# Linear attention and an ELU MLP on one core: a new order of the first loads, W1's first chunk by contraction tile, and a new order of all that follows

## Chip, cores and metric

One Trainium2 chip, one core. The metric is the device time of one execution in microseconds (us); every figure quoted as a time is the median of a kernel's runs. The span in a profile runs from the first to the last instruction and is about 1.8 us shorter than the time. All timed runs told here were in the fast state (two kernels have a single execution, e11 and e12, whose state is unknown), and all gave correct results.

## The reference

```python
def _attn_ref(q, k, v):                       # 8 batches, 8 heads, 576 tokens, 64
    q_s = np.exp(q - max over head_dim);  q_s /= sum over head_dim
    k_s = np.exp(k - max over tokens);    k_s /= sum over tokens
    kv = np.einsum('bhsd,bhse->bhde', k_s, v)
    return np.einsum('bhsd,bhde->bhse', q_s, kv)

def _moe_ref(x, w_in, w_out):                 # x: 4608 x 512, 512 -> 2048 -> 512
    h = x @ w_in
    g = np.where(h > 0.0, h, np.exp(np.minimum(h, 0.0)) - 1.0)
    return g @ w_out
```

(Shortened; `x` is the attention output with the heads side by side.)

## The kernel before

The program is a list of operations with their dependences, and a table `ORDER` that fixes the order on each engine by operation numbers. Two "halves" (`n`, four heads each) make a batch, 512 tokens make a block of the MLP. A "pitch" is the time from the start of one matmul to the start of the next, and "excess over the pitch" is what a start comes later than the usual pitch of its shape. Names: QS is exp(q) over its sum, qsT its transpose, VB the cast v, MBLK the normalised k-v product ("M"), XT the MLP's input (transposed attention output), GT the activated hidden layer, ESB its exponent, OSBX and OSB the outputs on their way out.

The start, and the loads of W1:

```python
        for n, t in ((0, "q"), (1, "q"), (0, "k"), (0, "v"), (1, "k"), (1, "v")):
            self.load(n, t, -40, "sp", follow=self.gpq)
            self.gpq = S.ops[-1]
            if (n, t) == (0, "k"):
                gate = S.ops[-1]
        loaded = S.ops[-1]
        for g0, g1, half in ((0, 3, 0), (0, 3, 1), (3, 5, None), (5, 8, None)):
            self.load_w1(g0, g1, half, -30, [gate, self.ident] if half == 0 else ())
            S.ops[-2].behind = loaded
        # ... stage1, transposes, k-v products, M for both halves ...
        self.side(C, -5, self.ao_mm(0, 0, C))      # product with M, one operation
        # ...
        for half in range(2):                      # MLP of block 0: contraction halves
            for g in range(3):
                self.hg_mm(0, g, turns[g], key, half)
```

Idle stretches of PE near the start are filled with spare matmuls on the identity, so that its clock "opens" early (the pitch of a spare matmul falls from 427 to 216 ns); their number comes from a schedule worked out when the kernel is built:

```python
                count = int((o.start - free - 150) / (430 if free == self.SPIN_FROM else 260))
```

The softmax here doesn't subtract the row's maximum and nothing guards it: scores larger than these inputs give would overflow.

## Time and profile before

| quantity, kernel before | value |
|---|---|
| time, 3 runs | 301.47 us (301.1 to 301.81) |
| span in the profile | 299.0 us |
| first MLP matmul (PS<-XT,W) | 14.95 us |
| first output matmul (PS<-W,GT), "first out" below | 30.70 us |
| from first out to the start of the last matmul | 265.02 us |

Up to first out lie the start, the MLP of block 0 and the loads of W1; after it everything else.

One stretch of PE's timeline (columns: start us, us, engine, line, operation, output<-inputs, size, count; in brackets idle time before it and what ended it), kernel before:

```profile
49.90 4.70 PE L547 MATMUL PS<-XT,W 128*128 128x512 f32 x20
54.98 1.19 PE L592 MATMUL PS<-W,GT 128*128 128x512 f32 x4 [0.39 <-DVE GT L582]
56.26 2.14 PE L547 MATMUL PS<-XT,W 128*128 128x512 f32 x8
```

PE stops before the four output matmuls because DVE has not yet written their GT. The gap over the usual pitch is 0.55 us here, and 0.25 more before the MLP matmuls at 56.26.

### The profile page before, as it was taken

The numbers are of one execution on the slowest core, as the hardware profiler recorded it, in microseconds if no ns is written. First come the engines' busy times: TensorE is split into PE (matmuls) and PEld (weight loads), VectorE is DVE, ScalarE is ACT, GpSimd is POOL, SyncE is SP. The second block draws the span as 40 slices with busy tenths as digits, with TensorE's granted clock in tenths as the row PEclk, the third lists the DMA queues.
The fourth block names the chain that finished last, engine by engine and source line by source line (L and its number), as shares of the span: only waits on it lengthen the run. The fifth ranks groups of instructions, "written<-read, shape, count | busy, mean of one in ns | idle before, by whom it ended". The sixth has DMA issues, their size and how long they took to land.

```text
span 299.0 us, 4421 instructions
## 1 busy us (share of the span) xinstructions
PE 287.1 (96%) x1851; PEld 234.5 (78%) x1851; DVE 189.5 (63%) x244; ACT 182.3 (61%) x212; POOL 21.7 (7%) x33
## 2 busy tenths in 40 slices
PE   0899999999999999999999999999999999999995
PEld 0487877677888888888888888888888888888885
DVE  3958935985898685894568855588427256655500
ACT  5858848988977967867755766534462423432411
POOL 0860145100000000000000000000000000000000
PEclk9999999999999999999999999999999999999999
DMA  7999998994498697289546327041312302004214
GB/s 260 387 398 389 390 391 262 240 371 157 118 247 259 141 338 181 71 263 266 175 116 164 88 66 186 2 99 37 86 36 51 70 2 53 0 0 107 64 41 105
DMA packets 35443, 49.96 MB, mean 167 GB/s; under 512 B 16352, under 2 KB 16608, under 8 KB 35424
## 3 DMA queue, kind: packets, MB, share of 16 engines
q1 hardware_dynamic: 29840, 34.15, 41.3%
q0 software_dynamic: 5504, 15.47, 16.3%
q8 instruction: 14, 0.23, 0.3%
q10 hardware_dynamic: 80, 0.07, 0.1%
q14 instruction: 5, 0.04, 0.1%
HBM read 36.70 MB, written 9.44 MB: 154 GB/s over the span
## 4 chain that ended last, share of the span: by engine, by line
PE 89%; DVE 4%; DMA 3%; ACT 1%; SPq 1%; issue 0%
PE PS L592 43%; PE PS L547 41%; PE PS L491 3%; DMA QT<-QS 2%; PE PS L460 2%; DMA QR<-in_q_dram 1%; DVE ZQ L376 1%; DVE QS L384 1%; PE PS L407 1%; SPq L634 1%; DVE XT L516 0%; DVE GT L582 0%; ACT QR L356 0%; ACT qsT L435 0%; ACT ESB L563 0%; DVE MBLK L473 0%
## 5 line engine op out<-in xcount | busy, mean ns | idle before, releaser
L592 PE MATMUL PS<-W,GT 128*128 128x512 f32 (+1 forms) x592 | 141.4, 386 | 0.4 <-DVE GT L582 0.4
L547 PE MATMUL PS<-XT,W 128*128 128x512 f32 x576 | 140.5, 391 | 0.7 <-DVE RZK L469 0.5
L547 PEld LDWEIGHTS PS<-XT,W 128*128 128x128 f32 x576 | 107.1, 188 | 24.0 <-DVE XT L516 0.9
L592 PEld LDWEIGHTS PS<-W,GT 128*128 128x128 f32 x592 | 107.7, 188 | 22.1 <-DVE GT L582 0.8
L563 ACT ACTIVATE ESB<-PS 128x1024 f32<-128x1024 f32 x72 | 73.7, 1027 | 64.7 <-PE PS L547 64.3
L580 DVE TENSOR_SCALAR ESB<-ESB 128x1024 f32<-128x1024 f32 x64 | 44.4, 695 | 67.0 <-ACT ESB L563 66.4
L582 DVE TENSOR_TENSOR GT<-ESB,PS 128x1024 fp32r<-128x1024 f32 x64 | 77.7, 1217 | 1.8
L624 ACT ACTIVATE OSB<-PS 128x512 f32<-128x512 f32 x31 | 18.2, 598 | 30.9 <-PE PS L592 30.6
L376 DVE TENSOR_REDUCE ZQ<-QR 128x18 f32<-128x1152 f32 x16 | 21.5, 1344 | 7.3 <-ACT QR L356 7.2
L513 ACT ACTIVATE XT<-PS 128x512 fp32r<-128x512 f32 (+6 forms) x32 | 19.5, 608 | 7.0 <-PE PS L491 6.5
L384 DVE TENSOR_TENSOR QS<-QR,RZQ 128x1152 f16<-128x1152 f32 x16 | 21.6, 1353 | 0.3
L356 ACT ACTIVATE QR<-QR 128x1152 f32<-128x1152 f32 x16 | 18.6, 1165 | 2.9 <-DMA QR<-in_q_dram 2.9
L360 ACT ACTIVATE KR<-KR 128x1152 bf16<-128x1152 f32 x16 | 18.5, 1160 | 3.0 <-DMA KR<-in_k_dram 3.0
L435 ACT ACTIVATE qsT<-QT 128x1152 fp32r<-128x1152 f16 x12 | 14.0, 1166 | 0.7 <-DMA QT<-QS 0.7
L369 ACT ACTIVATE VB<-VR 128x1152 bf16<-128x1152 f32 (+1 forms) x12 | 13.5, 1124 | 0.7 <-DMA VR<-in_v_dram 0.7
L491 PE MATMUL PS<-qsT,MBLK 128*128 128x320 f32 (+5 forms) x64 | 13.9, 303 | 0.0
L491 PEld LDWEIGHTS PS<-qsT,MBLK 128*128 128x128 f32 x64 | 11.7, 190 | 2.6 <-DVE MBLK L473 0.2
L576 DVE SCALAR_TENSOR_TENSOR GT<-PS,ESB 128x1024 fp32r<-128x1024 f32 x8 | 9.8, 1220 | 4.2 <-ACT ESB L574 4.2
L672 PE MATMUL PS<-ID 128*128 128x512 f16 x7 | 3.3, 590 | 7.5 <-ACT QR L356 7.5
L473 DVE TENSOR_TENSOR MBLK<-PS,RZK 64x128 fp32r<-64x128 f32 x32 | 9.2, 289 | 0.9
L574 ACT ACTIVATE ESB<-ESB 128x1024 f32<-128x1024 f32 x8 | 8.5, 1060 | 0.2
L469 DVE RECIPROCAL RZK<-PS 128x2 f32<-128x2 f32 x16 | 2.6, 164 | 8.7 <-PE PS L460 7.7
(29 smaller groups left out, 59.7 us busy)
## 6 DMA issues: line engine op xcount, KB each, us to landing
out_dram<-OSB SPq DMA_DIRECT2D x62, 128.0 KB, 2.4
QR<-in_q_dram SPq DMA_DIRECT2D x12, 576.0 KB, 5.3
KR<-in_k_dram SPq DMA_DIRECT2D x12, 576.0 KB, 5.6
VR<-in_v_dram SPq DMA_DIRECT2D x12, 576.0 KB, 5.6
W<-in_moe_w_out_dram POOLq DMA_DIRECT2D x4, 1024.0 KB, 18.9
QR<-in_q_dram POOLq DMA_DIRECT2D x4, 576.0 KB, 11.4
KR<-in_k_dram POOLq DMA_DIRECT2D x4, 576.0 KB, 11.6
VR<-in_v_dram POOLq DMA_DIRECT2D x4, 576.0 KB, 8.0
```

The lines of the kernel that those rows point to most:

```text
L356: S.add("act", t_act(1152, False), lambda e: e.activation(flat(q), flat(q), AF.Exp), key - 3, X=[f"qR{i}"], follow=self.table)
L360: S.add("act", t_act(1152, False), lambda e: e.activation(ek[:, :, :, :].rearrange("p h c d -> p (h c d)"), flat(k), AF.Exp), key - 2, X=[ ...
L376: S.add("dve", t_dve(1152), lambda e: e.tensor_reduce(self.ZQ[i][:, :, :].rearrange("p h c -> p (h c)"), q[:, :, :, :].rearrange("p h c d ...
L384: S.add("dve", t_dve(1152), lambda e: e.tensor_tensor(qso, q[:, :, :, :], rz, ALU.mult), key - 3, R=[f"qR{i}", f"RZQ{i}"], W=[f"QS{self.al ...
L491: last = e.matmul(P[:, y:y + n_], M[:, f, :], T[:, c0:c1, f * 64:f * 64 + 64], start=True, stop=True)
L513: S.add("act", t_act((h1 - h0) * n_, True), lambda e, dst=dst, src=src: e.activation(dst, src, AF.Copy), key, W=W, X=X)
L547: last = e.matmul(P[:, t * 512:(t + 1) * 512], self.W1[:, kc, tt * 128:(tt + 1) * 128], self.XT[:, kc, rc:rc + BLK], start=(kc == 0), stop ...
L563: S.add("act", t_act(1024, True), lambda e: e.activation(esb[:, :], P[:, :], AF.Exp), key, W=[f"E{i}"], X=banks)
L580: S.add("dve", t_dve(1024, 2), lambda e: e.tensor_scalar(esb[:, :], esb[:, :], 1.0, -1.0, ALU.min, ALU.add), key, X=[f"E{i}"])
L582: S.add("dve", t_dve(1024), lambda e: e.tensor_tensor(gt, esb[:, :], P[:, :], ALU.max), key, R=[f"E{i}"], W=gw, X=banks)
L592: last = e.matmul(dst, GT[:, jj, ts * 128:(ts + 1) * 128], self.W2[:, jj, c0:c1], start=(jj == 0), stop=(jj == 15))
L624: S.add("act", t_act(512, True), lambda e: e.activation(osb[:, :], src, AF.Copy), key, W=[f"O{i}0", f"O{i}1"], X=[f"b{bk}"])
```

## The change

Its intent: let the k-v product of half 0 start earlier (k second instead of third), and let the MLP begin on the first quarter of W1's first chunk instead of its first half. With both, all later orders were drawn up anew, so `ORDER` differs nearly everywhere. Core of the diff:

```diff
     "sp": (
-        "8 9 10 11 12 13 170 187 161 164 171 185 165 190 200 168 162 199 209 210 216 167 219 277 278 "
+        "8 9 10 11 12 13 197 178 195 171 172 181 200 180 177 175 209 219 210 174 220 226 229 325 287 "
 ... (all five engines' tables are new; numbers from about 50 on are shifted)
-        for n, t in ((0, "q"), (1, "q"), (0, "k"), (0, "v"), (1, "k"), (1, "v")):
+        for n, t in ((0, "q"), (0, "k"), (1, "q"), (0, "v"), (1, "k"), (1, "v")):
...
-            if (n, t) == (0, "k"):
+            if (n, t) == (1, "q"):
                 gate = S.ops[-1]
-        for g0, g1, half in ((0, 3, 0), (0, 3, 1), (3, 5, None), (5, 8, None)):
-            self.load_w1(g0, g1, half, -30, [gate, self.ident] if half == 0 else ())
+        for g0, g1, kcs in ((0, 3, (0,)), (0, 3, (1,)), (0, 3, (2, 3)), (3, 5, range(4)), (5, 8, range(4))):
+            self.load_w1(g0, g1, kcs, -30, [gate, self.ident] if kcs == (0,) else ())
...
-        self.side(C, -5, self.ao_mm(0, 0, C))
+        self.ao_parts(0, C, -5)
...
-        for half in range(2):
+        for kc in range(4):
             for g in range(3):
-                self.hg_mm(0, g, turns[g], key, half)
+                self.hg_mm(0, g, turns[g], key, kc=kc)
```

`ao_parts` issues the two matmuls of the product with M as two operations, so each releases its copy alone. The six first loads have the operation numbers 8 to 13 in both kernels.

## The prediction

> **What bounds the kernel now.** I read four views, from coarse to fine: the page's busy times, the busy table by stretches of time, then the timelines of PE and DVE for the first 17 us, and last the weight transfers from issue to landing.
>
> The page and the table by stretches (columns: stretch, its length, PE busy with its instructions, granted clock, DMA share, GB/s):
>
> ```profile
> PE 287.1 (96%) x1851; PEld 234.5 (78%) x1851; DVE 189.5 (63%) x244; ACT 182.3 (61%) x212; POOL 21.7 (7%) x33
> ...
> 14.95:24.75 9.80, 9.80 (x42) 1.00 1.30 397
> 24.75:30.33 5.58, 5.58 (x25) 1.00 1.24 388
> 30.33:46.95 16.62, 16.62 (x124) 1.00 1.13 379
> 46.95:60.00 13.05, 12.58 (x157) 1.00 0.98 242
> 60.00:76.00 16.00, 15.91 (x70) 1.00 0.71 245
> 76.00:100.00 24.00, 24.00 (x179) 1.00 0.75 197
> ```
>
> PE bounds it: idle for 299.0 - 287.1 = 11.9 us, of which 7.46 lie before its first instruction and 3 behind its last. From the first MLP matmul (14.95) to the last one PE has under 1 us of idle time. So the time is nearly "start of the MLP plus a fixed amount of PE work", and a change of the start moves the end one to one unless something else holds PE later. The second thing to see is the last column: up to 46.95 the transfers run at 379 to 397 GB/s, that is saturated too.
>
> The start, on PE:
>
> ```profile
> 7.46 2.31 PE L672 MATMUL PS<-ID 128*128 128x512 f16 x5 [7.46 <-ACT QR L356]
> 10.12 1.14 PE L407 MATMUL PS<-ID,QS 128*128 128x128 f16 x9 [0.34 <-DVE QS L384]
> 11.19 0.71 PE L460 MATMUL PS<-VB,KR 64*64 64x65 bf16 x36
> 11.83 0.61 PE L672 MATMUL PS<-ID 128*128 128x512 f16 x1
> 12.23 1.02 PE L407 MATMUL PS<-ID,QS 128*128 128x128 f16 x9
> 13.93 0.48 PE L460 MATMUL PS<-VB,KR 64*64 64x65 bf16 x36
> 14.95 1.17 PE L547 MATMUL PS<-XT,W 128*128 128x512 f32 x4 [0.53 <-DVE RZK L469]
> ```
>
> and on DVE:
>
> ```profile
> 10.27 1.36 DVE L384 TENSOR_TENSOR QS<-QR,RZQ 128x1152 f16<-128x1152 f32 x1
> 11.95 0.17 DVE L469 RECIPROCAL RZK<-PS 128x2 f32<-128x2 f32 x1 [0.32 <-PE PS L460]
> 12.16 0.61 DVE L473 TENSOR_TENSOR MBLK<-PS,RZK 64x128 fp32r<-64x128 f32 x2
> 12.80 0.76 DVE L372 CAST VB<-VR 128x576 bf16<-128x576 f32 x1
> 13.59 0.69 DVE L417 CAST qsT<-PS 128x512 fp32r<-128x512 f16 x1
> 14.20 0.68 DVE L516 CAST XT<-PS 128x512 fp32r<-128x512 f32 x1
> ```
>
> From QS of half 1 (ready at 11.63) DVE works almost without a gap until the XT copy at 14.88. The weights (issue, then the time to landing of those issued in a stretch):
>
> ```profile
> 8.41 5.08 POOL L336 DMA_DIRECT2D W<-in_moe_w_in_dram x8 [6.58 <-DMA KR<-in_k_dram]
> ...
> W<-in_moe_w_in_dram POOLq DMA_DIRECT2D x1, 384.0 KB, 5.2
> ...
> PEld PS L547 <- DMA W<-in_moe_w_in_dram: 0.3, 1, 0.3
> ```
>
> The first half of W1's first chunk lands at 8.41 + 5.2 = 13.6; the trace's landing records give 14.86 for the second half, which the first MLP matmul also needs. So two things release it within 20 ns: W1 at 14.86 and XT on DVE at 14.88 (the releaser in brackets, RZK, is only the last event on that counter). The last line is the load of W1's last columns: its record ends at 24.71, and PE starts on them at 24.75, with one pitch of 0.337 instead of 0.227 us. The input loads land at 4.69, 6.22, 8.11, 9.62, 11.11 and 12.61, about 1.5 us each (576 KB).
>
> **What the Trainium skill says.** "TensorE: Matmul & The Clock Gate", Part 1: the array runs at 1.2 GHz until a free-running activity window of about 3.4 us has been busy, then at 2.4; N=512 has a pitch of 426.7 ns cold and 215.7 warm, and the moment varies with the window's phase. The trace agrees: the first five filler matmuls on ID have a pitch of 427 ns, transposes 107 ns up to 12.87 and 57 ns after it. The f32r MLP matmuls have 227, not 216. The same page's table of specifications calls the queues of ScalarE, VectorE and GpSimdE strict FIFO; the DVE rows above are in program order throughout. "DMA: Bandwidth & Descriptors", Queues, rings and completion order: each DMA engine takes turns between the rows that have work, so an order inside one queue decides only who comes first, not how much is moved. The trace agrees: 390 to 406 GB/s whatever is under way. The Specifications there give 435 GB/s as the fabric's ceiling; no stretch of this trace goes above 412.
>
> **The change part by part.**
>
> Order q, k, q, v, k, v. The sixth transfer still lands at 12.61 and W1 is still gated on the third, so its issue stays at 8.41. k of half 0 takes the slot 6.22 and q of half 1 the slot 8.11. With ACT's 1.16 a pass: exp k0 6.25 to 7.41, exp q1 8.14 to 9.30. On DVE, QS of half 0 no longer stands behind the second reduce: reduce 5.91 to 7.26, reciprocal to 7.57, QS to 8.95 (before 10.06), 1.1 us sooner. But it buys nothing: the k-v product of half 0 needs the cast of v0, which still ends at 9.64 + 1.17 = 10.81. QS of half 1 is reduce 9.33 + 1.34, reciprocal 0.27, multiply 1.36, with 0.03 hops: 12.37, before 11.63. So 0.7 us are lost on the DVE queue, which was half of what set the start.
>
> DVE after that. The built order is RZK, MBLK first part, qsT copy, MBLK second part, V cast, XT copy. With the durations above: RZK 12.40 to 12.57, MBLK 12.60 to 12.88; the qsT copy needs the four transposes of half 1, which now come first in that group: 12.43 plus four pitches and a drain, about 12.85 at best. So 12.91 to 13.60, MBLK 13.63 to 13.92, V cast 13.95 to 14.70, XT 14.74 to 15.42. The k-v product of half 1 needs that cast and stands ahead of the MLP: 14.76 plus 0.35. First MLP matmul at best at about 15.1: 0.15 later than now.
>
> Filler matmuls. There are 12 now instead of 7: 3 before the transposes of half 0, 3 after them, 3 after the first k-v product, 3 after the transposes of half 1. Cold each takes 0.427, and they are in order with the real work. If the clock opens at 12.87 again: transposes from 9.01 to 9.97, three fillers to 11.27, k-v product from 11.4 (ready at 10.86) to 12.04, three fillers to 13.1; the transposes of half 1, ready at 12.43, start at 13.13, 0.7 late. The qsT copy then starts at 13.56 instead of 12.91, and everything behind it by as much: MLP at about 15.8. If the clock opens before about 11.6, the fillers fit and it stays 15.1. The opening could be anywhere from about 10 to 13.3 (window's phase), so on average about 0.25 us on top of the 0.15.
>
> W1 by contraction tile. First chunk now 2 x 192 KB, landing by about 13.6 instead of 14.86: 1.25 us won on the wait for weights, but off the path as DVE is later. The product with M in two parts lets ACT start its XT copy one pitch sooner (0.31), also beside the longer DVE chain. Two more descriptors' issues cost POOL 2 x 0.63 us, hidden: the last W1 is issued at 12.84 and lands 11.9 us later.
>
> End of W1. All bytes up to W1's last are the same, so it lands at about 24.7 again. Now PE meets it with 0.04 us to spare and loses 0.11 in the longer pitch. A later start regains that 0.11; an earlier one would wait there. Sum for the start: + 0.15 + 0.25 - 0.1 = + 0.3.
>
> The rest. The order of everything later is a new table (W2's chunks now come in pairs between the loads of q; the second block's first 32 MLP matmuls run in one piece). It moves no work in or out. The excess over the pitch between 46.95 and 76 is about 2 us in the trace (0.55 at 54.98, 0.25 at 56.26, 0.26 at 65.69, 0.16 at 74.35, and 0.11 at some restarts), so this can give or take some 0.5; I take 0 to - 0.1 for it.
>
> **The rivals.** (1) The intended gain in full: W1 1.25 us sooner gives an MLP start at 13.7. Against it: the DVE chain, and W1's last columns at 24.71, which would take it back; for the time it is worth 0.1 at most, 301.3. (2) Fillers cold to the end: + 0.9, 302.4. For it: the window in the trace before opened only at 12.87. (3) The new order of the middle wins or loses more than the start: 300.7 to 302.2; the DVE waits there are the only idle time left.
>
> **Range and chances.** 301.47 + 0.3 - 0.05 gives 301.7. The runs before spread by 0.7, the fillers by 0.9, the middle by about 0.5 each way: 8 in 10 from 300.8 to 302.6. Two per cent are 6 us, which nothing here reaches: faster 0.01, same 0.98, slower 0.01.
>
> **What would show it.** QS of half 1 ready at about 12.4; the qsT copy before MBLK's second part; first MLP matmul between 15.1 and 15.9 and released by the k-v product or XT, with W1's first tile landed at about 13.6; no longer pitch at W1's last columns, which land at about 24.7. I am wrong if the MLP starts before 14.9, if W1's last lands much before 24.7, or if the middle's PE waits change by more than 0.5 us.

## More of the kernel before

The output tiles of block 0 (OSBX) lie inside the buffer GT1, which block 1 writes, so a write of GT has to wait for the stores that still read it:

```python
        self.GT.append(a("GT1", [128, 16, BLK], F32R))
        # ...
        self.OSB0 = [at(f"OSBX{i}", [128, 512], F32, offset=base + 24576 + 2048 * i)
        # ...
        gw = [f"G{j % 2}_{g}"] + (self.early(g) if j == 1 else [])   # waits for OSBX's stores
```

The profiled execution took 300.83 us, less than any of the three timed ones.

## The result, and the profile after

The changed kernel took 300.68 us (300.4 to 301.11, 6 runs); the kernel before took 301.38 (6 runs) in the same comparison. The ratio is 0.9976, 95% interval 0.9963 to 0.9989. Ratios here are the mean time of one kernel's runs over that of the other's runs of the same rounds, so not quite the ratio of the medians. All outputs are right. It is within 2%, as predicted, but it is a small gain where a small loss was expected, and 300.68 lies just below the range (300.8 to 302.6).

The profiled execution happened to be the slowest of the six (span 299.3, before 299.0), so the profile cannot show the gain by its length. It is read by parts. The page of the changed kernel:

```profile
PE 287.9 (96%) x1856; PEld 234.4 (78%) x1856; DVE 187.5 (63%) x244; ACT 181.3 (61%) x212; POOL 22.8 (8%) x35
```

Five matmuls more are the five fillers more, two POOL instructions more are the two issues of W1. PE's timeline of the changed kernel up to the MLP:

```profile
8.93 1.14 PE L408 MATMUL PS<-ID,QS 128*128 128x128 f16 x9
9.86 1.49 PE L687 MATMUL PS<-ID 128*128 128x512 f16 x3
11.28 0.71 PE L461 MATMUL PS<-VB,KR 64*64 64x65 bf16 x36
11.93 0.85 PE L687 MATMUL PS<-ID 128*128 128x512 f16 x3
12.68 0.68 PE L408 MATMUL PS<-ID,QS 128*128 128x128 f16 x9
13.20 0.81 PE L687 MATMUL PS<-ID 128*128 128x512 f16 x3
14.19 0.73 PE L504 MATMUL PS<-qsT,MBLK 128*128 128x512 f32 x2 [0.18 <-DVE MBLK L474]
14.98 0.48 PE L461 MATMUL PS<-VB,KR 64*64 64x65 bf16 x36
15.39 0.50 PE L562 MATMUL PS<-XT,W 128*128 128x512 f32 x1
```

and DVE's:

```profile
11.26 1.36 DVE L385 TENSOR_TENSOR QS<-QR,RZQ 128x1152 f16<-128x1152 f32 x1
12.54 0.17 DVE L470 RECIPROCAL RZK<-PS 128x2 f32<-128x2 f32 x1
12.74 0.28 DVE L474 TENSOR_TENSOR MBLK<-PS,RZK 64x128 fp32r<-64x128 f32 x1
13.12 0.69 DVE L418 CAST qsT<-PS 128x512 fp32r<-128x512 f16 x1
13.84 0.29 DVE L474 TENSOR_TENSOR MBLK<-PS,RZK 64x128 fp32r<-64x128 f32 x1
14.16 0.76 DVE L373 CAST VB<-VR 128x576 bf16<-128x576 f32 x1
```

The transposes of half 0 come at 8.93 instead of 10.12, as intended. But half 1's QS ends at 12.62 (11.63 before), because its q now lands third, and then the DVE queue runs on without a gap: the V cast, the k-v product, the MLP at 15.39, which is 0.44 later than before. W1's first tiles landed at 13.38 and 13.84 and nobody waited for them.

The other end of the loads, from the table of waits of the changed kernel between 24 and 26 us (total, times, longest), and the stretch from there to first out (length, busy times of PE, PEld, DVE, ACT and POOL, clock, DMA share, GB/s):

```profile
PEld PS L562 <- DMA W<-in_moe_w_in_dram: 0.5, 1, 0.5
```

```profile
25.35:31.34 5.99, 5.95 (x28) 4.98 (x29) 4.87 (x6) 4.75 (x6) 0.00 (x0) 1.00 1.33 390
```

W1's last columns landed at 25.35 in this execution (24.70 and 25.16 in two others), and PE waited 0.26 us and 0.11 in a longer pitch. First out came at 31.34, 0.64 later than in the profile before. And yet the span is only 0.3 longer: the later work gave time back. PE's timeline of the changed kernel where the kernel before had its 0.55 us wait:

```profile
49.64 7.58 PE L562 MATMUL PS<-XT,W 128*128 128x512 f32 x32
57.06 2.06 PE L607 MATMUL PS<-W,GT 128*128 128x512 f32 x8
59.05 0.78 PE L461 MATMUL PS<-VB,KR 64*64 64x65 bf16 x72
```

All 32 MLP matmuls run in one piece and the eight output matmuls after them; GT is there in time, and there is no idle time before 57.06. The order has waits of its own for GT, though, as the next microseconds show:

```profile
60.11 3.94 PE L562 MATMUL PS<-XT,W 128*128 128x512 f32 x16 [0.28 <-DVE GT L597]
...
66.05 2.12 PE L562 MATMUL PS<-XT,W 128*128 128x512 f32 x8 [0.29 <-DVE GT L597]
```

They start 0.47 and 0.45 us over the pitch. The kernel before has no such wait near 60 and one of 0.26 at 65.69. So the 0.80 us of waits that went (0.55 and 0.25) were replaced in part.

### The profile page after: what moved, and what is told of

Same layout as the page of the kernel before. It is cut to its first block, busy times and chain, and to the rows that moved or that the text cites. A ratio compares the mean times of both kernels' runs of the same rounds, so it can differ in the third digit from the quotient of the medians.

```text
span 299.3 us, 4430 instructions
## 1 busy us (share of the span) xinstructions
PE 287.9 (96%) x1856; PEld 234.4 (78%) x1856; DVE 187.5 (63%) x244; ACT 181.3 (61%) x212; POOL 22.8 (8%) x35
## 3 DMA queue, kind: packets, MB, share of 16 engines
q0 software_dynamic: 5536, 15.47, 15.9%
## 4 chain that ended last, share of the span: by engine, by line
PE 84%; DMA 6%; DVE 4%; ACT 3%; POOL 2%; SPq 0%; issue 0%
PE PS L607 42%; PE PS L562 38%; DMA W<-in_moe_w_in_dram 4%; PE PS L492 2%; DMA QR<-in_q_dram 2%; POOL W L336 2%; PE PS L461 1%; DVE GT L597 1%; DVE GT L591 1%; ACT QR L357 1%; ACT OSBX L639 1%; DVE ESB L595 1%; DVE QS L385 0%; DVE ZQ L377 0%; ACT ESB L589 0%; DVE MBLK L474 0%
## 5 line engine op out<-in xcount | busy, mean ns | idle before, releaser
L526 ACT ACTIVATE XT<-PS 128x512 fp32r<-128x512 f32 (+6 forms) x32 | 19.4, 608 | 12.7 <-PE PS L492 7.7
L492 PEld LDWEIGHTS PS<-qsT,MBLK 128*128 128x128 f32 x60 | 11.0, 190 | 2.5 <-DVE MBLK L474 0.2
L492 PE MATMUL PS<-qsT,MBLK 128*128 128x320 f32 (+4 forms) x60 | 12.5, 296 | 0.0
L687 PE MATMUL PS<-ID 128*128 128x512 f16 x12 | 4.6, 508 | 7.3 <-ACT KR L361 7.3
L461 PEld LDWEIGHTS PS<-VB,KR 64*64 64x64 bf16 x576 | 5.7, 109 | 3.0 <-ACT VB L370 0.8
```

The lines of the kernel that those rows point to most:

```text
L492: last = e.matmul(P[:, y:y + n_], M[:, f, :], T[:, c0:c1, f * 64:f * 64 + 64], start=True, stop=True)
L526: S.add("act", t_act((h1 - h0) * n_, True), lambda e, dst=dst, src=src: e.activation(dst, src, AF.Copy), key, W=W, X=X)
```

## The experiments

To read them together, here is what the profile of each says of the two parts. "Runs" is the median of the timed runs, with their range; first out and "rest" (from first out to the last matmul's start) are from the trace.

| run | runs (us) | ratio to before, 95% | first MLP | first out | rest |
|---|---|---|---|---|---|
| before, medians in the comparisons | 300.91 to 301.38 | 1 | 14.95 | 30.70 | 265.02 |
| changed | 300.68 (300.4–301.11) | 0.9976 [0.9963, 0.9989] | 15.39 | 31.34 | 264.65 |
| e1 start only | 301.46 (301.18–301.85) | 1.0012 [0.9997, 1.0027] | 15.64 | 31.41 | 264.85 |
| e2 rest only | 300.33 (300.23–300.56) | 0.9972 [0.9956, 0.9987] | 14.99 | 30.63 | 264.80 |
| e3 before again | 301.01 (300.39–301.91) | 0.9996 [0.9978, 1.0013] | 15.10 | 30.77 | 265.16 |
| e4 changed again | 301.24 (300.40–302.32) | 1.0004 [0.9982, 1.0027] | 15.35 | 30.90 | 264.77 |
| e5 tiles and rest | 300.40 (299.87–300.73) | 0.9971 [0.9955, 0.9987] | 14.27 | 30.67 | 264.67 |
| e6 loads and rest | 301.06 (300.57–301.26) | 0.9995 [0.9981, 1.0009] | 15.16 | 30.82 | 264.64 |
| e7 rest on PE, DVE, ACT | 309.68 (308.18–310.01) | 1.0273 [1.0249, 1.0297] | 14.84 | 30.48 | 272.60 |
| e8 rest on POOL | 302.06 (301.43–303.99) | 1.0043 [1.0014, 1.0071] | 14.83 | 30.49 | 266.43 |
| e9 fewer fillers | 300.96 (300.34–301.80) | 0.9996 [0.9975, 1.0017] | 15.08 | 30.68 | 264.64 |
| e10 rest on all but POOL | 300.67 (300.36–301.05) | 0.9979 [0.9964, 0.9995] | 14.92 | 30.55 | 265.35 |
| e11, e12 before, one look each | 300.88, 300.88 | – | 15.00, 14.93 | 30.66, 30.53 | 265.12, 265.24 |
| e13 before, early fillers | 301.26 (300.22–302.29) | 1.0002 [0.9978, 1.0027] | 15.29 | 30.89 | 265.55 |
| e14 changed, early fillers | 300.56 (300.07–301.11) | 0.9982 [0.9964, 1.0] | 14.52 | 30.19 | 264.78 |
| e15 changed, third time | 300.94 (300.66–301.24) | 0.9994 [0.9976, 1.0012] | 15.67 | 31.24 | 264.77 |
| e16 rest only again | 300.45 (300.20–300.61) | 0.9978 [0.9962, 0.9993] | 14.87 | 30.81 | 264.63 |
| e17 one store earlier | 301.38 (300.64–301.47) | 1.0009 [0.9996, 1.0022] | 14.72 | 30.36 | 265.18 |
| e18 the same store later | 302.82 (301.98–304.80) | 1.0057 [1.0044, 1.0071] | 15.21 | 30.86 | 268.79 |

### e1 and e2: the two halves of the change alone, with e3 and e4 as controls

The theory after the result: the start costs what was predicted, and the new order of the rest gives more than predicted. Its rival: the start does not cost, and the order of the rest is neutral. e1 takes the changed kernel and puts the rest of each engine's table back into the order of before; e2 takes the kernel before and gives the rest the new order.

```diff
 e1 (changed kernel; "pe", behind the start, and so on every engine):
-        "138 146 147 140 148 117 141 149 119 160 159 136 161 144 166 142 168 162 167 150 169 163 156 "
+        "138 146 147 140 148 117 141 149 119 161 162 160 136 144 159 142 166 167 168 150 183 156 163 "
 e2 (kernel before; "sp" as an example, and so on every engine):
-        "8 9 10 11 12 13 170 187 161 164 171 185 165 190 200 168 162 199 209 210 216 167 219 277 278 "
+        "8 9 10 11 12 13 187 168 185 161 162 171 190 170 167 165 199 209 200 164 210 216 219 315 277 "
 e3: the kernel before, e4: the changed kernel, unchanged but for the label
```

> The changed start (load order, W1 and M by tile, its order up to the last MLP matmul of block 0), with the order of before for all that follows. Theory 'middle' (the start costs some 0.3 us, the new order of the rest gives 1 us back): 301.4 to 301.9, that is 0 to +0.5 against before, and the first MLP matmul at about 15.4 as in the changed kernel. Theory 'start' (the typical run of before starts its MLP later than the profiled one, because W1 lands later): 300.5 to 300.9, as the changed kernel.

> The start of before untouched, with the changed kernel's order for all that follows. Theory 'middle': 300.3 to 300.8, 0.6 to 1.1 below before, the first MLP matmul at about 15.0, the excess of PE over its pitch between 47 and 76 us down from 2.0 to about 1.2. Theory 'start': 301.2 to 301.5, no gain.

> The kernel before once more, for a second profile. Both theories: 301.1 to 301.8, ratio 1. If the landing of W1 varies from run to run (theory 'start'), the first MLP matmul comes later here than 14.95, up to 15.5; if not, at 14.9 to 15.0 again.

> The changed kernel once more, for a second profile. Both theories: 300.4 to 301.0. Theory 'start': first MLP matmul at 15.1 to 15.6 whatever W1 does, and W1's last columns land anywhere between 24.6 and 25.4, with a wait of PE there only when late. Theory 'middle': excess over the pitch between 47 and 76 us about 1.2 again.

Measured: e1 301.46 against 301.33 of before in its rounds, e2 300.33. The start alone is 0.12% slower (interval -0.03% to 0.27%) and the rest alone 0.28% faster (interval 0.13% to 0.44%, which is 0.85 us). That speaks for the theory. But e4, the whole change, came out at 301.24 and ratio 1.0004: its six runs were 300.4, 300.48, 300.75, 301.73, 302.05 and 302.32. So the 0.24% of the first comparison was not the end of the matter, and e15 below was needed.

PE's timeline of e1 shows why its MLP starts even later than in the changed kernel: the clock opened later, and the fillers before the transposes ran cold at a pitch of 0.427 until 12.7.

```profile
14.44 0.73 PE L504 MATMUL PS<-qsT,MBLK 128*128 128x512 f32 x2 [0.18 <-DVE MBLK L474]
15.23 0.48 PE L461 MATMUL PS<-VB,KR 64*64 64x65 bf16 x36
15.64 1.66 PE L562 MATMUL PS<-XT,W 128*128 128x512 f32 x6
```

And e2's, at the wait in the middle:

```profile
48.93 7.59 PE L546 MATMUL PS<-XT,W 128*128 128x512 f32 x32
56.36 2.04 PE L591 MATMUL PS<-W,GT 128*128 128x512 f32 x8
```

With the start of before and the new order, the pause before the output matmuls is gone here too. The wait after the output matmuls, at 59.40 here, is the new order's own. The starts of all matmuls, each against the median pitch of its shape, give the balance: between 47 and 61.5 us the excess is 2.06 to 2.21 us in the four profiles of before and 1.65 to 1.79 in those of the changed kernel, e2 and e16. From 61.5 us on these two groups do not differ clearly (4.2 to 4.5 and 4.3 to 4.5).

### e5 and e6: W1 by tile alone, the load order alone

Both have the new rest. e5 has the loads and the start order of before with W1, the product with M and the first MLP matmuls by tile; e6 has the new load order with its start order and W1 as before.

```diff
 e5 (changed kernel, start order of before):
-        for n, t in ((0, "q"), (0, "k"), (1, "q"), (0, "v"), (1, "k"), (1, "v")):
+        for n, t in ((0, "q"), (1, "q"), (0, "k"), (0, "v"), (1, "k"), (1, "v")):
-            if (n, t) == (1, "q"):
+            if (n, t) == (0, "k"):
 e6 (kernel before, start order of the changed kernel, new rest):
-        for n, t in ((0, "q"), (1, "q"), (0, "k"), (0, "v"), (1, "k"), (1, "v")):
+        for n, t in ((0, "q"), (0, "k"), (1, "q"), (0, "v"), (1, "k"), (1, "v")):
-            if (n, t) == (0, "k"):
+            if (n, t) == (1, "q"):
```

> Loads and start order of before, W1's first load and the first M and MLP products by tile, and the changed kernel's order for the rest. If the last columns of W1 are a floor (they land at 24.2 to 24.7 whatever the start does), the first MLP matmul comes at 14.4 to 14.6 instead of 15.0, PE waits 0.2 to 0.5 us at those columns, and the time is that of the rest alone: 300.2 to 300.5. If they are no floor, the 0.5 us come through: 299.8 to 300.0.

> Load order q, k, q, v, k, v with its order of the start, W1 and M in the pieces of before, and the changed kernel's order for the rest. If the load order is what the start loses by (DVE chain 0.7 us later), the first MLP matmul comes at 15.3 to 15.9 and the time is 300.6 to 300.9, 0.3 to 0.5 above the rest alone. If the loss is from something else (fillers of the changed start are also here, so only the tiles are left), MLP at 15.0 and 300.3.

e5, PE's timeline and its waits between 24 and 26 us:

```profile
14.27 1.49 PE L562 MATMUL PS<-XT,W 128*128 128x512 f32 x4
15.73 0.73 PE L504 MATMUL PS<-qsT,MBLK 128*128 128x512 f32 x2
16.29 14.18 PE L562 MATMUL PS<-XT,W 128*128 128x512 f32 x60
...
30.67 1.63 PE L607 MATMUL PS<-W,GT 128*128 128x512 f32 x6
```

```profile
PEld PS L562 <- DMA W<-in_moe_w_in_dram: 0.4, 1, 0.4
```

and e2's PE in the same stretch:

```profile
14.99 1.20 PE L546 MATMUL PS<-XT,W 128*128 128x512 f32 x4 [0.54 <-DVE XT L515]
16.02 0.63 PE L490 MATMUL PS<-qsT,MBLK 128*128 128x512 f32 x2
16.49 13.94 PE L546 MATMUL PS<-XT,W 128*128 128x512 f32 x60
```

These are the two floors that rival (1) of the prediction named, the DVE chain and W1's last columns, and most of the gain goes at the first. The MLP starts 0.72 us earlier than in e2 (14.27 against 14.99), but the fifth MLP matmul only 0.20 earlier (16.29 against 16.49): the first four are held on the way (W1's second tile landed at 14.79, DVE's XT copy ended at 14.95), and the product with M of half 1 waits for MBLK, which DVE finishes at 15.67 here and 15.66 in e2. Just before W1's last columns PE is 0.25 ahead (24.34 against 24.59); it stands before them until 24.72, as they landed at 24.68, and the rest is gone. First out is 30.67 against e2's 30.63: nothing of the 0.72 is left. The times agree (300.40 and 300.33). W1 by tile is worth nothing while DVE's chain and the last load end where they did.

e6 took 301.06 against e2's 300.33, so the load order, with the start order and the 12 fillers that go with it, costs about 0.7 in the timed runs (all six of e6 lie above all five of e2); in its profile, which was the fastest of its runs (300.57), first out is only 0.19 later than e2's. The cost of this start is therefore shown in sign, and in size only between those two.

### e7, e8 and e10: which engine's order matters

The rest's new order on some engines alone, each on the kernel before.

```diff
 e7:  "pe", "act", "dve" get the new rest; "sp" and "gp" stay
 e8:  "gp" (POOL's transfers) gets the new rest; all others stay
 e10: "pe", "act", "dve", "sp" get the new rest; "gp" stays
```

> Start of before, new order of the rest on PE, DVE and ACT only; the transfers in the order of before. If the gain of the middle comes from PE's order (32 MLP matmuls in one piece before the first product that needs GT), it is here in full: 300.2 to 300.6 and the wait of 0.55 us at 55 is gone. If it comes from the order of the transfers, it is not: 301.0 to 301.4.

> Start of before, order of before on PE, DVE, ACT and SP; only the transfers issued by POOL (q, W2 in pairs, v, k) in the new order. PE's order theory: 301.0 to 301.5 and the wait of 0.55 us at 55 still there. Transfers' theory: 300.3 to 300.7.

> Start of before; new order of the rest on PE, DVE, ACT and SP; only POOL's transfers in the order of before. If the 8 us that the new engine order lost at 114 with the old transfers came from SP's queue (a store of the output standing behind loads there), they are gone: 300.3 to 300.7, the gain of the middle without the new order of W2. If POOL's order was it: 305 or more.

e7 lost 8 us. Its wait at 55 us is gone, but PE and ACT stand still later:

```profile
113.83 3.78 PE L591 MATMUL PS<-W,GT 128*128 128x512 f32 x8 [5.68 <-ACT OSB L623]
```

```profile
113.19 0.60 ACT L623 ACTIVATE OSB<-PS 128x512 f32<-128x512 f32 x1 [6.54 <-DMA out_dram<-OSB]
```

ACT cannot empty a PSUM bank because an output buffer is still being stored, and PE waits for the bank; its granted clock was 0.85 in the 12 us that follow. e10 differs from e7 by SP's order alone and does not have this wait, so the stores in SP's old order were too late for the new order of the engines. e8 lost 0.43%: PE waited 1.2 us for ACT's XT copy at 45.02, and the wait of 0.55 us ahead of the output matmuls was still there. It goes with the orders of PE, DVE and ACT, which e7 changed together. e10 came to 300.67, near e2, though on another chip. (Its profiled execution was its slowest, 301.05, with PE idle for 0.33 us before 43.23, waiting for a chunk of W2, hence the rest of 265.35.) The orders of the engines and of SP belong together, and what POOL's adds is not separated by the intervals.

### e9, e13 and e14: fillers

The spread of e4 could come from the phase at which PE's clock opens. e9 leaves out the three fillers after the first k-v product; e13 and e14 start the fillers at about 2 us in the kernel before and the changed kernel, so that the clock is open before the real work.

```diff
 e9 (changed kernel):
-                if count > 0:
+                if count > 0 and o.idx != 47:
 e13 (kernel before), e14 (changed kernel):
-    SPIN_FROM = 7900.0
+    SPIN_FROM = 2600.0
```

> The changed kernel without the three filler matmuls between the first k-v product and the transposes of half 1. If these fillers, cold in the runs where the clock opens late, are what the changed start loses by and what spreads its runs (300.4 to 302.3), the time is 300.3 to 300.6 and the runs lie within 0.5 us. If their work is to open the clock sooner, it is 300.9 or more, with the first MLP matmuls at the cold pitch of 0.43 us.

> The kernel before with 18 filler matmuls from about 2.6 us on instead of 5 from 7.5, so that the clock opens before any real product. If the spread of before (300.4 to 302.0) is the moment of opening, the runs lie within 0.4 us, the transposes of half 0 have the pitch of 57 ns, and the median is 300.8 or less. If not, spread and median are as before: 301.1 to 301.4.

> The changed kernel with 15 fillers from 2.6 us on. If the moment of opening is its spread (300.4 to 302.3), the runs lie within 0.4 us, the first MLP matmul is at about 15.1 (my best case, the fillers between no longer cold) and the median 300.4 or less. If not, 300.7 to 301.3 with the old spread.

e9: 300.96, from 300.34 to 301.80, so the spread stayed; those fillers are not its cause. e13 and e14: the transposes ran at a pitch of 57 ns, and the times were 301.26 and 300.56, with spreads of 2.1 and 1.0. An open clock does not take the spread away. e13's MLP still started at 15.29, because W1's second half landed only at 15.20. e14's loads landed early in its profile (the first MLP matmul is at 14.52), and its first out, 30.19, is the earliest of all. Its ratio of 0.9982 has an interval up to 1.0, so no gain of the early fillers over the changed kernel is shown.

e13's profiled execution was one of its slower ones (301.55), and it caught something, on DVE and on PE:

```profile
73.78 1.23 DVE L575 SCALAR_TENSOR_TENSOR GT<-PS,ESB 128x1024 fp32r<-128x1024 f32 x1 [2.98 <-DMA out_dram<-OSBX]
```

```profile
75.06 1.20 PE L591 MATMUL PS<-W,GT 128*128 128x512 f32 x4 [0.75 <-DVE GT L575]
```

The write of GT waited for the last store of OSBX, which landed at 73.70, and PE for GT, 0.91 us over its pitch. In all profiles with SP's old order the store landed at 72.0 to 73.7, and in the four of the kernel before PE's wait there was at most 0.16. In the new order it landed at 69.5 to 70.7.

### e11, e12, e15 and e16: more looks

The same kernels again: before twice (one look each), the changed kernel, and the rest alone.

> The kernel before, one more profile, to see a run above 301.2: all profiles of before so far were of its faster runs (300.83, 301.03). If its slow runs lose in the middle, the waits of PE between 47 and 77 us add up to more than 2.1; if they lose at the start, the first MLP matmul is later than 15.1.

> The same once more, with the same two readings: waits of PE between 47 and 77 us above 2.1 us (middle), or a first MLP matmul after 15.1 (start).

> The changed kernel once more. If the gain measured first (0.9976) is real, 0.997 to 0.999 of before, median 300.5 to 300.9; if the second measurement (1.0004) is the rule, 1.000 and about 301.2.

> The new rest on the start of before, once more and on the chip of the three runs above: 300.3 to 300.7, ratio about 0.997 to 0.998, within 0.5 us from run to run; below the changed kernel by 0.2 to 0.5, which is what its start costs.

e11 and e12 were to catch a slow run of before; both took 300.88, so neither did. e16 repeats e2 (300.45, ratio 0.9978); the eleven runs of this kernel lie between 300.20 and 300.61. e15 gives the changed kernel a third comparison: 300.94, ratio 0.9994. It ran in the same rounds as e16, from which it differs by the start alone, and all its runs (300.66 to 301.24) lie above all of e16's: with the new rest the start costs about 0.5 us here. Over its three comparisons (0.9976, 1.0004, 0.9994) the changed kernel gained between 0.7 us and nothing.

### e17 and e18: one store

Theory A, from e13: the remainder of the rest's gain, and the spread of the kernel before, come from that late store. Theory B: the store has nothing to do with it. SP's issues, before:

```profile
64.52 0.58 SPq L319 DMA_DIRECT2D QR<-in_q_dram  x1
65.15 0.47 SPq L319 DMA_DIRECT2D VR<-in_v_dram  x1
65.66 0.49 SPq L634 DMA_DIRECT2D out_dram<-OSBX  x1
```

and of the changed kernel:

```profile
65.41 0.49 SPq L649 DMA_DIRECT2D out_dram<-OSBX  x1
65.93 0.58 SPq L320 DMA_DIRECT2D QR<-in_q_dram  x1
```

Before, the store stands behind two loads of 576 KB and landed at 72.17; in the changed kernel it stands ahead of them and landed at 70.67.

```diff
 e17 (kernel before, "sp"):
-  ... 209 210 216 167 219 ...
+  ... 209 167 210 216 219 ...
 e18 (e2, "sp"):
-  ... 209 200 164 210 216 219 ...
+  ... 209 200 210 216 164 219 ...
```

> The kernel before with one instruction moved: on SyncE's queue the last store of block 0's output is issued ahead of the loads of q and v of its neighbourhood instead of behind them. All other orders as before. Theory A (the late store is what the slow runs of the kernel before lose by, through the write of GT that waits for it): landing at about 70 us instead of 72.2 to 73.7, runs within 0.5 us of each other, median 300.8 (the rest's -0.7 to -1.0 less the 0.55 that the MLP order wins at 55 us), so ratio about 0.998. Theory B (the store has nothing to do with it; all of the gain is the order of the MLP matmuls): 301.1 to 301.4 as the kernel before, runs 300.3 to 302, the PE wait near 75 us at most 0.16.

> The start of the kernel before with the new order of the rest, and only that store moved back behind the loads of q and v, as before has it. Theory A: landing at 72 to 73.7 us, runs spread by 1 us and more, median 300.7 to 301.0 instead of 300.33 and 300.45. Theory B: 300.3 to 300.5 with a spread of 0.4, as the two runs of that order.

e17's store was issued at 64.45 and landed at 69.29, as intended, and the time did not move: 301.38, ratio 1.0009. Theory A falls for the kernel before. Its wait ahead of the output matmuls is still there:

```profile
54.68 1.20 PE L592 MATMUL PS<-W,GT 128*128 128x512 f32 x4 [0.38 <-DVE GT L582]
```

e18 is slower than either theory said, 302.82. Its profiled execution was its slowest, 304.80, so what follows is larger there than in its other runs. SP's issues, then DVE and PE of e18, then two stretches of its table (columns as above):

```profile
65.58 0.46 SPq L318 DMA_DIRECT2D QR<-in_q_dram  x1
67.52 0.37 SPq L318 DMA_DIRECT2D VR<-in_v_dram  x1
67.93 0.49 SPq L633 DMA_DIRECT2D out_dram<-OSBX  x1
```

```profile
73.65 1.22 DVE L581 TENSOR_TENSOR GT<-ESB,PS 128x1024 fp32r<-128x1024 f32 x1 [2.90 <-DMA out_dram<-OSBX]
```

```profile
74.92 1.65 PE L546 MATMUL PS<-XT,W 128*128 128x512 f32 x3 [2.53 <-DVE GT L581]
```

```profile
71.00:80.00 9.00, 6.47 (x22) 4.86 (x21) 2.36 (x2) 5.47 (x7) 0.00 (x0) 0.81 0.34 113
80.00:100.00 20.00, 20.00 (x160) 16.63 (x159) 15.79 (x23) 15.54 (x19) 0.00 (x0) 1.00 0.72 211
```

Here the load of v in front of the store was itself held until 67.52, and the store behind it in the same queue with it. It landed at 73.62, GT waited 2.90 us and PE 2.69 over its pitch, and the eight matmuls after the pause ran at a pitch of 0.427 (granted clock 0.81 in that stretch): some 1.6 us more. In the new order the store's place ahead of the loads is needed; in the old one it is not what the time is lost by.

## Why the prediction was wrong, and where it was right

**The start: right in its mechanism, a little short.** QS of half 1 was ready at 12.62 (predicted 12.4), the qsT copy came before MBLK's second part, W1's first tile landed at 13.38 and 13.84 (predicted 13.6), and the first MLP matmul was released behind the k-v product at 15.39, 15.35 and 15.67 (predicted 15.1 to 15.9). The sum of + 0.3 was a bit low: first out came at 31.34, 30.90 and 31.24 against 30.70, 30.77, 30.66 and 30.53 in four profiles of before, means 31.16 and 30.67, so + 0.5. Nearly all of it is there at the first MLP matmul (means 15.47 and 15.00), where the prediction had 0.15 + 0.25. The term that was meant to give back 0.1, the longer pitch at W1's last columns, did not: W1's last columns landed later in two of three profiles (25.35 and 25.16, predicted 24.7), and in the first PE waited for them; in e15 it came to them at 25.40 without a wait. The prediction also called W1's two more issues hidden. In the seven profiles with W1 by tile its last load was issued at 13.2 to 14.0 us and landed at 24.2 to 25.4, in the thirteen others at 12.4 to 13.3 and 23.9 to 24.8, so they may not be; no run tests it.

**Rival (1), the intended gain with its floors: right as a rival.** e5 shows both: 0.52 of its 0.72 us went by the fifth MLP matmul, with DVE's chain, and the rest at W1's last columns.

**Rival (2), fillers cold to the end:** seen in part. In e1 and e15 they were cold until 12.7 and the MLP came at 15.64 and 15.67, 7.37 and 7.28 us after W1's first issue; in the first profile of the changed kernel, where the clock opened near 12.1, and in e14, where it was open, it came 6.74 and 6.73 after it. So a late opening cost some 0.55 us, near the 0.7 between the prediction's two cases (15.1 and 15.8).

**The failed step is "The rest", which the prediction put at 0 to - 0.1.** In the profiles, first out to the last matmul took 265.02, 265.16, 265.12 and 265.24 before (mean 265.14) and 264.65, 264.77 and 264.77 in the changed kernel (mean 264.73): - 0.4. In the timed runs it was worth - 0.85 (e2) and - 0.7 (e16), the ratio times 301. The prediction saw the waits of 0.55 and 0.25 that it comes from, named the one piece of 32 MLP matmuls, and said that the whole "can give or take some 0.5". It then entered almost nothing for it. What it could have worked out from the built order: the output matmuls move behind eight more MLP matmuls, 8 x 0.227 = 1.8 us later, while their GT was late by 0.55; so that wait had to go, unless a new one came. Two new ones came, near 60 and 66 us (0.44 to 0.62 each in all profiles of the new order), against 0.21 to 0.34 near 66 or 71 before; with the one near 60 alone, 0.80 shrinks to 0.3, and the profiles show 0.4. Rival (3) was this case, with its lower end at 300.7.

**The sum in the profiles is + 0.5 - 0.4 = + 0.1**, which is what the spans say (299.3, 299.0, 299.3 against 299.0, 299.2, 299.1, 299.1). By the profiles the change is neutral. By the timed runs it gains from 0 to 0.7 us. That the first comparison fell below the range has a share of luck: the two repeats, 301.24 and 300.94, lie inside it. The starting point, 301.47, was the median of three runs; six gave 301.38, later ones 300.91 to 301.33. One reading of the lines was too neat, without effect on the sum: "390 to 406 GB/s" leaves out the 379 and 388 of the prediction's own table.

**What stays open.** About 0.3 to 0.45 us of the rest's gain appears only in timed runs: 0.7 to 0.85 there against 0.4 in the profiles. The kernel before and the changed kernel spread by 1.5 and 1.9 us in e3 and e4, while e2 and e16 spread by 0.3 and 0.4; slow timed runs of these kernels have no trace. The gap lies in which executions were profiled: the four of before took 300.83 to 301.03, each below the median of before in its comparison, those of e2 and e16 300.56 and 300.55, above theirs. So the profiled executions themselves differ by only 0.35 us. What makes the slower runs of before slow was not found. For the changed kernel the start is a part: its profiles of 301.11 and 301.11 have first out at 31.34 and 31.24, the one of 300.75 at 30.90. Three of the fillers (e9), the clock (e13, e14) and the late store of before (e17) were tried and are not the cause. Also, the effects did not add: e1 and e2 sum to - 0.16%, e4 of the same rounds measured + 0.04%, which their intervals allow. One reason is in e1's profile: behind the later start the old order lost less (rest 264.85, and 0.58 us over the pitch between 61.5 and 77 us against 0.78 to 0.99 in the profiles of before), so a part of the start's + 0.5 to + 0.7 came back in the old order. The new order keeps its waits near 60 and 66 behind either start; that this is why nothing comes back there is argued, not shown. So the exact net gain of the change isn't settled. What is settled is the sign of the rest's gain, the sign of the start's cost in the new order (e15 against e16, e6 against e2; in the old order e1's interval includes no cost), and that the rest alone, with the start of before, is the better kernel: e2 and e16 lie 0.2 to 0.3% below the kernel before with intervals that exclude 1, though nowhere near 2%. The variants with the load order of before and the whole new rest are the best ones measured (e2, e5 and e16: 300.33 to 300.45).

## What to carry to other kernels

Where a change to one stage brings a newly drawn-up order for everything, price the order as a part of its own: list the waits of the profile that sit on the bound engine, ask of each whether the new order still has its cause, and look for the waits that it makes. A faster start is worth nothing if the next links of the chain, or the last load, end when they did. A store whose buffer is reused soon can cost much behind a load that can itself be held (e18), and next to nothing elsewhere (before against e17).

## What the Trainium skill lacked or had wrong

- "TensorE: Matmul & The Clock Gate", Part 1, gives a pitch of 215.7 ns for N=512 warm and has no figure for f32r operands. The f32r matmuls here have 227 ns throughout; the f16 fillers have 216 to 217.
- The same page has the transition to the full clock "around 4µs into sustained matmul activity, ±500ns run-to-run". Counted from PE's first matmul it took 5.4 us in the profile before (7.46 to 12.87), 5.0 in e3 (7.36 to 12.3) and between 3.5 and 4.1 in e17 (7.36 to 10.8 or 11.5). The activity here had gaps (PE idle 0.34 us before 10.12), so this is a case that the page gives no figure for, and no disproof.
- No page I found has the price of the first matmul after a wait, or of one released just in time: its pitch was 0.335 to 0.341 us instead of 0.227 at 24.75, 54.98 and 56.26 in the profile before and at 60.11 and 66.05 in the changed kernel's.
- "DMA: Bandwidth & Descriptors", Queues, rings and completion order, tells how queues take turns but gives no figure for a place in a queue. The same store of 128 KB landed 4.0 to 5.4 us after its issue ahead of two loads of 576 KB (e2, changed kernel, e17 and others), and 6.5 to 7.6 us behind them in before, e1 and e13, but 6.1, 5.7 and 4.5 us behind them in e8, e18 and e7, so these runs give no fixed price either.
